# A fixed instruction order for every engine, with gated weight loads, an interleaved head and an unequal last tile

## The chip, the cores and the metric

The kernel runs on one core of a Trainium2 chip. The metric is the device time of that core in microseconds (us), lower is better. A kernel is timed in several executions; I quote the median and the range.

TensorE is called PE below, ScalarE is ACT, VectorE is DVE, GpSimd is POOL and SyncE is SP. "Full" matmuls use the whole 128x128 array. "Tiled" matmuls use it as four independent strips: the score fills take four heads side by side in four row strips, the products with the probabilities take them in four column strips.

## The reference, cut to what matters

The input x is 2048 x 512 in bf16. Two branches are mixed by a gate per token.

```python
g = sigmoid((x * gate_w).sum(-1, keepdims=True))
a = A(x, wq, wk, wv, wo, beta)          # 32 heads of 16, 4 segments of 512 tokens
b = (gelu(x @ w_gate) * (x @ w_up)) @ w_down     # 512 -> 1792 -> 512
return g * a + (1 - g) * b

# A, for each segment s of 512 tokens:
p = softmax(q_s @ k_s.T * scale + causal_mask)
a_dot = p @ v_s
a_mem = (phi(q_s) @ M) / (phi(q_s) @ z + 1e-6)   # memory of the earlier segments
o = sigmoid(beta) * a_mem + (1 - sigmoid(beta)) * a_dot
M += phi(k_s).T @ v_s;  z += phi(k_s).sum(tokens)
# A ends with o @ wo
```

Attention needs many exponentials on ACT (64 of 128x2048 elements and 8 for the low part of the mask) and, with 16 columns per head, tiled matmuls. The projections and branch B are full matmuls that fill the time between.

Of the kernel before, what the change touches and what calls it, by code (L numbers as in the profile page):

```python
# [32 lines left out]
PV_JOIN = 0.11  # L33
HOLD = 0.3
OPEN_BONUS = 6.0
BIAS = {
    "D0": -705, "D1": -805, "D2": -380, "D3": -442, "G0": -222, "G1": -900, "G2": -744, "G3": -86, "GdT0": 97,
    "GdT1": 844, "GdT2": -1, "GdT3": 895, "Gev0": 862, "Gev1": -349, "K0": 777, "K1": -529, "K2": 250,
    "K3": 307, "Q0": 715, "Q1": -519, "Q2": 584, "Q3": -641, "U0": -844, "U1": -888, "U2": -53, "U3": -206,
    "Um0": 900, "Um1": 148, "Um2": 49, "Um3": -86, "V0": 318, "V1": -357, "V3": 539, "Vev0": 540, "Vev1": 758,  # L40
    "Vev2": 262, "Vev3": -72, "Vlo0": -900, "Vlo1": 900, "Vlo2": -70, "Vlo3": 237, "consts": 21, "exp0": -666,
    "exp1": 177, "exp2": -517, "exp3": -395, "exsT0": 77, "exsT1": -899, "exsT2": -94, "exsT3": 695, "fin0": 37,
    "fin1": -471, "fin2": 741, "fin3": -517, "gbd": -146, "gelu0": -795, "gelu1": 416, "gelu2": 1, "gelu3": 126,
    "gexp": 402, "gexs0": -594, "gexs1": -701, "gexs3": 76, "gmat": -900, "gmul1": 900, "gmul2": -10,
    "gmul3": 319, "gsum0": -318, "gsum1": -86, "gsum2": -613, "gsum3": -900, "gts0": 73, "gts1": -850,
    "gts2": -487, "gts3": 848, "ident": 503, "kl0": -826, "kl1": -900, "kl2": -661, "kl3": 900, "kp0": 509,
    "kp1": 3, "kp2": -900, "kp3": -405, "masks": 769, "msk0": -290, "msk1": 789, "msk2": 116, "msk3": -63,
    "mz0": -162, "mz1": 638, "mz2": -319, "mzacc0": -423, "mzacc1": 170, "mzacc2": 439, "mzbd0": -25,
    "mzbd1": -178, "mzbd2": 70, "norm0": 704, "norm1": -880, "norm2": -46, "norm3": 166, "num2": -887,
    "num3": -200, "nump1": -900, "nump2": -220, "nump3": -164, "oTd1": 896, "oTd2": 268, "oTd3": 899,  # L50
    "omg": 528, "out0": 408, "out1": -644, "out10": 2, "out11": 869, "out12": 745, "out13": 461, "out14": -25,
    "out15": -280, "out2": 230, "out3": -27, "out4": 313, "out5": -134, "out6": 284, "out7": -18, "out8": 682,
    "out9": -139, "pkT0": 5, "pkT1": 569, "pkT2": 281, "pkc0": 489, "pkc1": -900, "pkc2": -14, "pke0": 310,
    "pke1": 399, "pke2": -73, "pqc1": 496, "pqc2": 14, "pqc3": -117, "pqe1": -17, "pqe2": 649, "pqe3": 63,
    "pv0": -95, "pv1": -551, "pv2": -900, "pv3": 30, "pvt0": -169, "pvt1": 86, "pvt2": -513, "pvt3": -26,
    "qk0": 417, "qk1": 185, "qk2": 503, "qk3": 669, "tload": 355, "vones": -877, "w": -765, "warm0": 21,
    "warm1": 747, "warm2": -324, "warm3": 371, "warm4": 223, "warm5": -120, "warm6": -334, "x0": -96,
    "x0ev0": 93, "x0ev1": 23, "x0t0": 596, "x0t1": 606, "x1": 367, "x2": -181, "x3": -900, "xt1": 533,
    "xt2": -189, "xt3": 11
}  # L60
HOP = {PE: 0.17, ACT: 0.07, DVE: 0.07, POOL: 0.10, SP: 0.0}
# [40 lines left out]
class Task:  # L102


    def __init__(self, name, alts, grp=None, after=(), bias=0.0, nbytes=0):
        self.name = name
        self.alts = alts
        self.grp = grp
        self.after = tuple(after)
        self.bias = bias + BIAS.get(name[:re.search(r"[_.]|$", name).start()], 0.0)  # L110
        self.nbytes = nbytes
        self.tiled = None
        self.patience = 0.0
        self.ahead = False
        self.est = {e: sum(i.est for i in l) for e, l in alts.items()}
        rs, ws = set(), set()
        for l in alts.values():
            for i in l:
                rs.update(i.reads)
                ws.update(i.writes)  # L120
        self.reads, self.writes = rs, ws
        self.preds, self.succs = set(), set()
        self.prio = 0.0
        self.eng = None
        self.start = self.finish = None
        self.id = None


class Sched:
# [32 lines left out]
    def schedule(self):  # L162
        tasks = self.tasks
        n = len(tasks)
        groups = defaultdict(list)
        for t in tasks:
            if t.grp is not None:
                groups[t.grp].append(t)
        for g in groups.values():
            for t in g[1:]:  # L170
                for d in () if t.ahead or PE in t.alts else t.preds:
                    if d.grp is not g[0].grp and d not in g[0].preds:
                        g[0].preds.add(d)
                        d.succs.add(g[0])
        indeg = [len(t.preds) for t in tasks]
        topo = [t for t in tasks if indeg[t.id] == 0]
        for t in topo:
            for s in t.succs:
                indeg[s.id] -= 1
                if indeg[s.id] == 0:  # L180
                    topo.append(s)
        assert len(topo) == n, "cycle"
        for t in reversed(topo):
            best = max([s.prio for s in t.succs] + [0.0])
            t.prio = min(t.est.values()) + best + t.bias
        npred = [len(t.preds) for t in tasks]
        ready_at = [0.0] * n
        ready = {e: set() for e in ENGINES}
        for t in tasks:
            if npred[t.id] == 0:  # L190
                for e in t.alts:
                    ready[e].add(t)
        cur = {e: 0.8 for e in ENGINES}
        bank_free = {b: 0.0 for b in range(self.nbanks)}
        dma_free = 0.0
        order = []
        last_pe = None
        while len(order) < n:
            best = None
            due = min([ready_at[t.id] for t in ready[ACT] if t.tiled == "exp"] + [1e9])  # L200
            held = sum(t.tiled == "pv" and ready_at[t.id] <= cur[PE] + HOLD for t in ready[PE])
            for e in ENGINES:
                for t in ready[e]:
                    st = max(cur[e], ready_at[t.id])
                    if e == ACT and t.tiled != "exp" and st + t.est[e] > due + 0.1:
                        continue
                    if t.tiled == "pv":
                        if last_pe in ("qk", "pv") and ready_at[t.id] <= cur[e] and bank_free and \
                                min(bank_free.values()) <= cur[e]:
                            if best is None or (-1.0, 0.0, t.id) < best[0]:  # L210
                                best = ((-1.0, 0.0, t.id), e, t)
                            continue
                        st += t.patience
                    if t.grp is not None and t.grp.bank is None:
                        if len(bank_free) <= (0 if t.tiled == "pv" else held):
                            continue
                        st = max(st, min(bank_free.values()))
                    open_ = t.grp is not None and t.grp.bank is not None
                    k = (st, -t.prio - (OPEN_BONUS if open_ else 0.0), t.id)
                    if best is None or k < best[0]:  # L220
                        best = (k, e, t)
            assert best is not None, "deadlock in task graph"
            (st, _, _), e, t = best
            if t.tiled == "pv":
                st = max(cur[e], ready_at[t.id], min(bank_free.values()))
            for a in t.alts:
                ready[a].discard(t)
# [5 lines left out]
            if e == PE:  # L233
                if t.tiled == "pv" and last_pe == "pv":
                    t.finish -= PV_JOIN
                last_pe = t.tiled
# [14 lines left out]
            for s in t.succs:  # L251
# [3 lines left out]
                if npred[s.id] == 0:  # L255
                    for a in s.alts:
                        ready[a].add(s)
# [116 lines left out]
def _build(es, nc, A_x, A_wq, A_wk, A_wv, A_wo, A_beta, B_w_gate, B_w_up, B_w_down, gate_w, out):  # L374
# [108 lines left out]
    rank = [9000.0]  # L483

    def xk(s, kb):

        return [("xT", s % NX, kb, u) for u in range(2)]

    def wdma(key, eng, dst, src, nbytes, nonc=False, after=()):
        rank[0] -= 20.0  # L490
        dma("w_" + str(key), eng, lambda: dst, lambda: src, [], [("w", key)], nbytes, bias=rank[0], nonc=nonc,
            after=after)

    def xdma(s, after=()):
        for kb in range(4):
            rank[0] -= 20.0
            dma(f"x{s}_{kb}", SP, lambda kb=kb: xT[s % NX][:, kb, :],
                lambda kb=kb: A_x[0, s * 512:(s + 1) * 512, kb * 128:(kb + 1) * 128],
                [], xk(s, kb), 262144, issue=1.25, transpose=True, bias=rank[0] if s < 2 else 0.0,
                after=after)  # L500
# [10 lines left out]
              [("c", "ident")], [("c", "ident")], 0.3)], bias=9990.0)  # L511
    task("tload", ACT, [Instr(lambda e: e.activation(stmp[:, 0:1], ones[:, 0:1], ACTF.Exp), writes=[("stmp",)],
                              est=1.5)], bias=8000.0)
    xin = hT[1][:, 0:4, :]
    for a in range(4):
        rank[0] -= 20.0
# [612 lines left out]
```

## The kernel before: the parts that the change and the argument touch

The kernel first builds a graph of tasks, then gives each engine its list of instructions. A task names what it reads and writes; semaphores follow from that. Before the change a list scheduler picks the order, with a hand-tuned bias per kind of task.

```python
BIAS = {"D0": -705, "D1": -805, "D2": -380, ...}          # [cut: 175 such biases in all]

def schedule(self):                                        # [cut to the choice]
    for t in reversed(topo):
        t.prio = min(t.est.values()) + max([s.prio for s in t.succs] + [0.0]) + t.bias
    while len(order) < n:
        for e in ENGINES:
            for t in ready[e]:
                st = max(cur[e], ready_at[t.id])
                if t.tiled == "pv":       # joined with a fill or another pv where it can be
                    if last_pe in ("qk", "pv") and ready_at[t.id] <= cur[e] and bank_free and ...:
                        ...
                    st += t.patience
                k = (st, -t.prio - (OPEN_BONUS if open_ else 0.0), t.id)
                if best is None or k < best[0]:
                    best = (k, e, t)
```

A score fill is 8 tiled matmuls (32 small ones for the low part of the mask) that write four PSUM banks ("X"), which one exp on ACT then reads. There is only one such set of banks, so the next fill can't start before the exp of the last one has ended. I call the time from fill to fill, when nothing but the exp holds it up, the exp round trip.

```python
def fill(name, steps, dst, key, masks):
    for (lhs, rhs, c0, ncol, rd) in steps:
        for g in range(4):
            e.matmul(X[g][:, c0:c0 + ncol], lhs(32 * g), rhs(32 * g),
                     start=True, stop=True, tile_position=(32 * g, 0))       # L803
    e.activation(dst[:], XALL[:, :].rearrange("p (g c) -> p g c", g=4),
                 ACTF.Exp, scale=ATT_SCALE)                                  # L810
    e.affine_select(out=view, ...)                                           # L814, POOL, the causal mask
```

A probability-times-value group ("PV") is 16 tiled matmuls with Vaug (L852) and 16 small ones for the low part (L860). The memory update is 64 small tiled matmuls (L769). Fills use row strips, PV groups and the memory update use column strips, so that PE has three modes: full, rows, columns. Each full matmul comes from one helper, line L449, and most are cut into pieces of two matmuls of 512 columns. The loads at the start and the end of the kernel:

```python
for a in range(4):                       # x0 in four row blocks on two issuing engines
    dma(f"x0_{a}", (SP, ACT)[a % 2], ..., A_x[0, a * 128:(a + 1) * 128, :], ...)
for c0, c1 in ((0, 128), (128, 512)):    # wk and wq in two column blocks
    for key, w, src in (("wk", wk, A_wk), ("wq", wq, A_wq)):
        wdma((key, c0 > 0), SP, w[:, :, c0:c1], r4(src)[:, :, c0:c1], ...)
...
for part in (dwn, att):                  # the last output tile: two halves of 256 columns
    for u in range(2):
        c0 = 256 * u
        ins = [mm(None, lambda u=u: X[u][:, 0:256], a, b[:, c0:c0 + 256], ...) ...]
# half 0 is copied out by ACT, half 1 by DVE; both are stored by SP
```

The softmax here doesn't subtract the row's maximum and nothing guards it: scores larger than these inputs give would overflow.

## Time and profile before

| | before |
|---|---|
| time, median of three runs | 269.23 us (269.0 to 269.25) |
| profiled span | 267.5 us |
| PE busy | 257.9 us (96%) |
| ACT busy / DVE busy | 212.1 us (79%) / 199.9 us (75%) |
| chain of waits that ended last | 84% PE |
| first score fill starts | 16.84 us |
| last matmul starts to end of span | 2.91 us |

The first lines are from the page of the kernel before: busy times by engine (time, share of the span, instructions), then the shares of the chain of work that ended last, then two groups of instructions (line, engine, operation, tiles, shapes, count | busy time, mean ns of one | idle time just before them and what ended it).

```profile
PE 257.9 (96%) x2965; PEld 118.4 (44%) x3005; DVE 199.9 (75%) x385; ACT 212.1 (79%) x188; POOL 102.3 (38%) x232
...
PE 84%; ACT 5%; DVE 3%; issue 3%; DMA 2%; POOL 1%; SPq 0%; ACTq 0%; DVEq 0%
...
L810 ACT ACTIVATE pt<-psXALL 128x2048 bf16<-128x2048 f32 x64 | 120.1, 1876 | 26.0 <-PE psXALL L803 23.9
```

PE has 2965 matmul records and 3005 weight loads: 40 matmul records are missing in this trace. "Issue" is time in which an engine waits for nothing that the profile shows. The Trainium skill ("Perfetto Trace Analysis", Identifying the Most-Contended Engine) warns that the busy share of matmuls is a poor measure of how close a kernel is to its limit, since they are pipelined. So I read PE from the start-to-start times of its instruction records.

Here is the wait view of PE of the kernel before (engine, tile, line, what it waited for: us in total, times, longest; one line and the last are cut).

```profile
PE psW L449 <- issue: 3.8, 24, 0.2
...
PE psW L449 <- ACT qT L463: 0.4, 1, 0.4
PE psW L449 <- ACT hT L937: 0.4, 1, 0.4
PE psXALL L803 <- ACT pt L810: 0.3, 2, 0.2
PE psW L449 <- DMA wk<-in_A_wk_dram: 0.3, 1, 0.3
```

PE hardly waits for a named source. The first line is no wait: its gaps stand where matmul records of 0.216 us are missing. The two waits of 0.4 us have a missing record in them as well. And this is how dense it is, in a stretch of the timeline of the kernel before in the last segment (start us, us, engine, line, operation, count, and an idle time in brackets if there was one).

```profile
227.26 0.40 PE L803 MATMUL psXALL<-qT,kpad 32*128 32x320 bf16 x8
227.59 2.33 PE L449 MATMUL psW<-xT,wu 128*128 128x512 bf16 x10
229.85 0.40 PE L803 MATMUL psXALL<-qT,kpad 32*128 32x448 bf16 x8
```

From one fill to the next are 2.59 us: ten full matmuls of 512 columns, 216 ns each, and a fill that takes 428 ns in all. The columns of the fill explain about 213 of the 428 ns. The other 0.2 us are what it costs to enter the tiled mode and leave it again, so about 0.1 us a switch. From row strips to column strips is a switch too: a PV group alone between full matmuls takes 0.76 us (read in the new order's trace, where single groups occur), a fill alone 0.43 us, and the two joined 1.09 us, which is one switch less than the sum.

### The profile page before, as it was taken

The numbers are of one execution on the slowest core, as the hardware profiler recorded it, in microseconds if no ns is written. First come the engines' busy times: TensorE is split into PE (matmuls) and PEld (weight loads), VectorE is DVE, ScalarE is ACT, GpSimd is POOL, SyncE is SP. The second block draws the span as 40 slices with busy tenths as digits, with TensorE's granted clock in tenths as the row PEclk, the third lists the DMA queues.
The fourth block names the chain that finished last, engine by engine and source line by source line (L and its number), as shares of the span: only waits on it lengthen the run. The fifth ranks groups of instructions, "written<-read, shape, count | busy, mean of one in ns | idle before, by whom it ended". The sixth has DMA issues, their size and how long they took to land.

```text
span 267.5 us, 7093 instructions
## 1 busy us (share of the span) xinstructions
PE 257.9 (96%) x2965; PEld 118.4 (44%) x3005; DVE 199.9 (75%) x385; ACT 212.1 (79%) x188; POOL 102.3 (38%) x232
## 2 busy tenths in 40 slices
PE   8999999999999999999999999999999999999996
PEld 5444444344443443434354444444344444444354
DVE  1769799898989898889756877987952688753451
ACT  4889988899998997998858998887767767777602
POOL 8364553873002433485201433486300252352300
PEclk9999999999999999999999999999999999999999
DMA  6998992000203443000021224010020025001002
GB/s 192 228 328 184 390 241 42 1 2 0 44 0 79 81 101 102 22 20 2 0 44 39 42 59 124 21 44 2 0 44 0 2 59 42 0 22 36 8 0 78
DMA packets 33775, 18.22 MB, mean 68 GB/s; under 512 B 21456, under 2 KB 33744, under 8 KB 33744
## 3 DMA queue, kind: packets, MB, share of 16 engines
q1 hardware_dynamic: 33456, 17.51, 27.0%
q8 instruction: 23, 0.38, 0.6%
q10 hardware_dynamic: 288, 0.26, 0.3%
q14 instruction: 8, 0.07, 0.1%
HBM read 9.84 MB, written 2.10 MB: 45 GB/s over the span
## 4 chain that ended last, share of the span: by engine, by line
PE 84%; ACT 5%; DVE 3%; issue 3%; DMA 2%; POOL 1%; SPq 0%; ACTq 0%; DVEq 0%
PE psW L449 68%; PE psXALL L803 8%; PE psW L852 5%; ACT pt L810 3%; DMA wk<-in_A_wk_dram 2%; PE psXALL L449 1%; PE psW L860 1%; POOL exsT L712 1%; DVE tb L867 0%; PE psW L769 0%; ACT L937 0%; ACT L926 0%; SPq L480 0%; DVE mzbd L784 0%; DVE phkt L692 0%
## 5 line engine op out<-in xcount | busy, mean ns | idle before, releaser
L810 ACT ACTIVATE pt<-psXALL 128x2048 bf16<-128x2048 f32 x64 | 120.1, 1876 | 26.0 <-PE psXALL L803 23.9
L814 POOL TENSOR_SCALAR_AFFINE_SELECT pt<-pt 128x256 bf16<-128x256 bf16 x128 | 59.2, 464 | 131.6 <-ACT pt L810 126.6
L449 PE MATMUL psW<-xT,wu 128*128 128x512 bf16 x216 | 51.9, 380 | 0.8 <-issue 0.6
L449 PE MATMUL psW<-xT,wg 128*128 128x512 bf16 x214 | 50.2, 380 | 1.7 <-issue 1.3
L449 PE MATMUL psW<-wd,hT 128*128 128x512 bf16 x203 | 50.3, 380 | 0.9 <-issue 0.8
L958 DVE TENSOR_TENSOR hT<-psW,hT 128x512 bf16<-128x512 f32 x56 | 37.5, 684 | 11.4 <-PE psW L449 10.9
L449 PEld LDWEIGHTS psW<-xT,wg 128*128 128x128 bf16 x224 | 20.4, 98 | 25.7 <-issue 2.5
L449 PEld LDWEIGHTS psW<-xT,wu 128*128 128x128 bf16 x224 | 20.4, 98 | 24.5 <-issue 2.3
L867 DVE STREAM_TRANSPOSE tb<-psW 128x512 f32<-128x512 f32 x32 | 21.3, 697 | 12.6 <-PE psW L860 12.2
L449 PEld LDWEIGHTS psW<-wd,hT 128*128 128x128 bf16 x210 | 18.8, 98 | 22.5 <-issue 2.5
L803 PE MATMUL psXALL<-qT,kpad 32*128 32x320 bf16 (+3 forms) x512 | 25.8, 273 | 0.3 <-ACT pt L810 0.3
L937 ACT ACTIVATE hT<-psW 128x512 bf16<-128x512 f32 x28 | 15.9, 601 | 7.0 <-PE psW L449 6.9
L814 POOL TENSOR_SCALAR_AFFINE_SELECT ptl<-ptl 128x2048 bf16<-128x2048 bf16 x8 | 16.9, 2117 | 9.4 <-ACT ptl L810 9.0
L803 PEld LDWEIGHTS psXALL<-qT,kpad 32*128 32x128 bf16 x512 | 7.7, 92 | 27.6 <-ACT pt L810 19.6
L852 PE MATMUL psW<-pt,vaug 128*17 128x192 bf16 (+3 forms) x512 | 18.7, 273 | 0.0
L810 ACT ACTIVATE ptl<-psXALL 128x2048 bf16<-128x2048 f32 x8 | 15.0, 1876 | 3.6 <-PE psXALL L803 3.6
L449 PE MATMUL psW<-xT,wk 128*128 128x512 bf16 (+1 forms) x64 | 16.1, 376 | 0.8 <-issue 0.5
L712 POOL COPY exsT<-exs 32x4 f32<-32x4 f32 x64 | 15.4, 241 | 3.7
L466 DVE CAST hT<-psW 128x512 bf16<-128x512 f32 x21 | 14.1, 683 | 2.8 <-PE psW L449 2.5
L449 PE MATMUL psW<-wo,oT 128*128 128x512 bf16 x55 | 15.2, 380 | 0.5 <-issue 0.3
L449 PE MATMUL psW<-xT,wq 128*128 128x512 bf16 x60 | 14.9, 380 | 0.7 <-ACT qT L463 0.4
L449 PE MATMUL psW<-wv,xT 128*128 128x512 bf16 x62 | 15.0, 380 | 0.3 <-issue 0.3
(98 smaller groups left out, 300.0 us busy)
## 6 DMA issues: line engine op xcount, KB each, us to landing
out_dram<-ost SPq DMA_DIRECT2D x15, 128.0 KB, 1.7
wg<-in_B_w_gate_dram SPq DMA_DIRECT2D x2, 896.0 KB, 6.1
wu<-in_B_w_up_dram SPq DMA_DIRECT2D x2, 896.0 KB, 5.9
wd<-in_B_w_down_dram SPq DMA_DIRECT2D x1, 1792.0 KB, 12.1
phkt<-in_A_x_dram SPq DMA_DIRECT2D x3, 512.0 KB, 4.1
vlow<-vaug SPq DMA_DIRECT2D x8, 136.0 KB, 2.9
wv<-in_A_wv_dram SPq DMA_DIRECT2D x1, 512.0 KB, 6.2
wo<-in_A_wo_dram SPq DMA_DIRECT2D x1, 512.0 KB, 9.7
```

The source lines that it names most:

```text
L449: return Instr(lambda e: e.matmul(view(), lhsT, rhs, start=first, stop=last), reads=reads, writes=[fkey if fkey is not None else g.key], e ...
L466: alts[DVE] = [Instr(lambda e: e.tensor_copy(dst(), src()), reads=reads, writes=writes, est=dve_t(n))]
L712: cross = task(f"exsT{s}", POOL, [Instr(lambda e, g=g, c=c: e.tensor_copy(exsT[sl][32 * g:32 * g + 32, c:16:4], exs[32 * c:32 * c + 32, s4 ...
L803: instrs.append(Instr(lambda e, g=g, lhs=lhs, rhs=rhs, c0=c0, ncol=ncol: e.matmul(X[g][:, c0:c0 + ncol], lhs(32 * g), rhs(32 * g), start=T ...
L810: prev_exp[0] = exp_task(s, f"exp{s}_{t}{name}", [Instr(lambda e: e.activation(dst[:], XALL[:, :].rearrange("p (g c) -> p g c", g=4), ACTF ...
L814: task(f"msk{s}_{t}{name}", POOL, [Instr(lambda e, view=view, pat=pat, base=base: e.affine_select(out=view, in_=view, compare_op=ALU.is_ge ...
L852: instrs.append(Instr(lambda e, t=t, q=q, kb=kb, slot=slot, c0=c0: e.matmul(gp.f32()[32 * q:32 * q + 17, 128 * kb + 64:512], Vaug[sl][:, k ...
L860: instrs.append(Instr(lambda e, t=t, q=q, kb=kb, c0=c0: e.matmul(gp.f32()[32 * q:32 * q + 17, 128 * kb:128 * kb + 64], Vlow[j][:, kb, 4 * ...
L867: task(f"pvt{s}_{t}_{j}", DVE, [Instr(lambda e: e.transpose(Tb[:, j, :], gp.f32()[:, :]), [gp.key], [("Tb", j)], dve_t(512))], grp=gp)
L937: lambda e, g=g, ft=ft, s=s: e.activation(hT[s % 2][:, ft, :], g.f32()[:, :], ACTF.Gelu_apprx_tanh),
L958: task(f"Um{s}_{ft}", DVE, [Instr(lambda e, g=g, ft=ft: e.tensor_tensor(hT[sl][:, ft, :], g.f32()[:, :], hT[sl][:, ft, :], ALU.mult), [g.k ...
```

## The change

Its intent is to replace the scheduler, which guesses, by a fixed list for each engine that was searched for with a better model of PE: it charges each change of mode, a slow clock in the first 5.8 us, and instruction fetch in blocks of 256. The large weights get gates, so that their transfers do not collide with the start. The head is cut finer.

```diff
-PV_JOIN = 0.11
+SWITCH = 0.097
+COLD = 5.8
+BLOCK, BLOCK_ASK, BLOCK_END = 256, 165, 208
-BIAS = { ... }
+ORDER = {"pe": ("warm3 warm0 warm2 warm1 warm6 warm4 x0t0_0 x0t1_0 warm5 K0_0.0 ..."),
+         "act": (...), "dve": (...), "pool": (...), "sp": (...)}     # [cut: lists of all tasks]
 def schedule(self):
-        # list scheduling with priorities                              [cut]
+        named = {t.name: t for t in self.tasks}
+        queue = {e: [named[x] for x in reversed(ORDER[e].split())] for e in ENGINES}
+        # takes each queue in order; only assigns the PSUM banks       [cut]

-    for c0, c1 in ((0, 128), (128, 512)):        # wk, wq by columns, after all of x0
-        for key, w, src in (("wk", wk, A_wk), ("wq", wq, A_wq)):
-            wdma((key, c0 > 0), SP, ...)
+    x0dma(0)
+    x0dma(1)
+    for kb in range(4):                          # wk by row blocks, on SP and ACT in turn
+        wdma(("wk", kb), (SP, ACT)[kb % 2], wk[:, kb, :], A_wk[128 * kb:128 * kb + 128, :], ...)
+    x0dma(2)                                     # issued as x0_0, wk0, x0_2, wk2 (SP)
+    x0dma(3)                                     #       and x0_1, wk1, x0_3, wk3 (ACT)

-        pieces(name, g, [mm(...) ...], 2 * nu)
+        pieces(name, g, [mm(...) ...], 1 if nu == 2 else 2)   # K of segment 0: 256-column pieces
+        # Q of segment 0 is accumulated in the score banks X                    [cut]

-                masks = [(PTl[:]..., [[0, 32], [2, 64]], 1, 2048)]
+                masks = [(PTl[:, g, :]..., [[0, 8], [2, 64]], 1, 512) for g in range(4)]

-    wdma(("wu", 0), SP, wu[:, :, 0:half], wur[:, :, 0:half], 917504, after=pk0)
+        wdma(("wu", i), SP, wu[:, :, sl], wur[:, :, sl], 917504, reads=[("tick", 0, *e)])
+    # likewise x2, wd in two halves, wo: each waits for the exp after a named fill of segment 0

-                        c0 = 256 * u
+                        c0, cn = 384 * u, (384, 128)[u]                # last output tile
```

The cut leaves out that wq and wv come in two halves each, and that x1 is loaded ahead of the second half of wg. The new PE list differs from the old order above all in how PV groups are placed. The old kernel always put two of them behind one fill. The new list often puts a single one beside a fill. Here is a stretch of the last segment, a "piece" being two matmuls of 512 columns:

```
before: qk3_1B0 pv3_0_0 pv3_0_1 (2 pieces) qk3_1A1 (5 pieces) qk3_1B1
after:  qk3_1B0 (3 pieces) pv3_0_0 qk3_1A1 (3 pieces) pv3_0_1 qk3_1B1
```

Here the two fills with their PV groups have five switches before and six after.

## The prediction

> **What bounds the kernel.** TensorE, issue after issue. The page gives PE 96% busy, ACT 79%, DVE 75%; the chain of waits that ended last is 84% PE. By the start-to-start times of the instruction records, a 512-column matmul starts 216 ns after the last one from 7.24 us to the last matmul at 264.6 us. The rest is structural: a score fill (8 row-tiled matmuls) costs 428 ns between full matmuls, of which about 213 are its own columns. So entering or leaving the tiled mode costs about 0.1 us. A fill joined with two probability-times-value (PV) groups saves one such switch (1.87 us, separately 0.43 + 1.54). Real stalls after 7.24 us come to only about 0.6 us, two of them (0.22 and 0.35 us) waits for an exp on ACT. Outside: 7.24 us of head, including 2.8 us of warm-up matmuls and a 0.45 us pause for wk (landed 7.19 us), and 2.9 us of tail after the last matmul starts.
>
> **What the change does.**
> 1. Head: wk in four row blocks among the x0 loads. wk should be in by about 5.5 us instead of 7.2, so the 0.45 us pause goes. But one warm-up now stands between the transposes (0.43 us at half clock): net about -0.2 us. The Trainium skill ("TensorE: Matmul & The Clock Gate", Part 1) says the array runs at half clock for its first few busy microseconds; the trace agrees (transposes 107 ns apart, full clock from 6.45 us).
> 2. Order: the matmul columns stay the same. Counting the new PE list, there are 173 mode switches; in the old trace I count 165, since PV groups were always joined in pairs. 8 x 0.1 = +0.8 us.
> 3. The old stalls (-0.6 us at best) can go. But five of the new fill-to-fill periods hold only 2.15 to 2.34 us by my sum, less than the exp round trip (2.46 us), four in the last segment: up to +0.8 us of new waits on ACT.
> 4. Gated weights: wu, wd, wo later. Needed only from about 67 us: no cost. The intent seems to be instruction fetch; the skill ("Runtime: NRT & Kernel Launch", Instruction fetch mechanics) describes 16 KiB blocks of 256 instructions; the trace shows 23 such packets on an instruction queue, about 1 us each. I find no PE stall there, so nothing to win.
> 5. Tail: the last piece on PE is now 384 columns evacuated by ACT (about 0.58 us, between 0.47 for 256 and 0.69 for 512) instead of 256 on DVE (0.48): about +0.1 us.
>
> **Sum.** +0.1 to +0.9 us, against the hope that a list from a better model stalls less than I see. Prediction 269.3 us, range 268.2 to 270.9. Faster by over 2%: 0.01; within 2%: 0.96; slower: 0.03.
>
> **What would show each step.** The first K projection matmul near 5.0 us and no wait on wk; PE work done by 12 us about 0.2 us ahead; 216 ns and 428 ns slots unchanged; PE waits on exp in the last segment's fills; last matmul to end about 3.0 us.
>
> **What would make it wrong.** Full clock granted earlier or later than 6.45 us (half of any shift is gained or lost); the fixed order meeting a late transfer (second half of wg, x1 in the first 20 us), which stalls everything behind it; fetch stalls where 300 instructions of tiled work follow each other fast; a cheaper switch from PV to a fill.

## The result, and the profile after

| | before | after |
|---|---|---|
| time, median | 269.12 us (268.83 to 269.25, 4 runs) | 270.23 us (270.02 to 271.0, 4 runs) |
| profiled span | 267.5 us | 268.5 us |
| PE busy | 257.9 us (96%) | 263.2 us (98%) |
| first score fill starts | 16.84 us | 14.79 us |
| last matmul starts to end of span | 2.91 us | 3.13 us |

The first fill starts 2.05 us earlier, but that is not a gain of this size: the new list has six matmuls of V (1.3 us) behind the first fill that the old one had before it. The ledger below takes this into account.

The ratio is 1.0048, with a 95% interval from 1.0026 to 1.007: within 2%, but slower beyond the noise. Ratios here are the mean time of one kernel's fast runs over that of the other's fast runs of the same rounds, so they are not quite the ratio of the medians in the table.

The page of the kernel after, in the same order as above:

```profile
PE 263.2 (98%) x3017; PEld 118.9 (44%) x3017; DVE 199.4 (74%) x387; ACT 213.1 (79%) x188; POOL 106.4 (40%) x256
...
PE 88%; ACT 9%; DMA 1%; issue 1%; POOL 0%; SPq 0%; ACTq 0%
...
L871 ACT ACTIVATE pt<-psXALL 128x2048 bf16<-128x2048 f32 x64 | 120.0, 1875 | 23.5 <-PE psXALL L864 21.4
L875 POOL TENSOR_SCALAR_AFFINE_SELECT ptl<-ptl 128x512 bf16<-128x512 bf16 x32 | 23.0, 719 | 77.3 <-ACT ptl L871 75.7
```

One exp still takes 1.88 us. (Most of the 5 us more of PE busy are the records that were missing before.) What is new is ACT in the chain: 9% instead of 5%. The wait view of PE of the kernel after:

```profile
PE psXALL L864 <- ACT pt L871: 0.8, 3, 0.3
PE psW L498 <- DMA wk<-in_A_wk_dram: 0.2, 1, 0.2
```

The waits for the exp rose from 0.3 to 0.8 us, and this view counts only the larger ones. Where they sit is plain in the chain of the kernel after, between 221 and 230 us (start us, us, what):

```profile
221.83 0.44 PE psXALL L864 x8
...
222.35 1.89 ACT pt L871
...
224.28 0.50 PE psXALL L864 x8
...
224.87 1.89 ACT pt L871
...
226.80 0.51 PE psXALL L864 x8
...
227.39 1.89 ACT pt L871
```

The chain goes from exp to fill to exp, every 2.52 us, and leaves the full matmuls out: this is the exp round trip. In the kernel before, the same chain from 223.91 us on runs through PE alone. The timeline of the kernel after shows why:

```profile
224.28 0.40 PE L864 MATMUL psXALL<-qT,kpad 32*128 32x320 bf16 x8 [0.17 <-ACT pt L871]
224.61 1.04 PE L498 MATMUL psW<-xT,wu 128*128 128x512 bf16 x4
225.49 0.59 PE L498 MATMUL psW<-wd,hT 128*128 128x512 bf16 x2
226.01 0.61 PE L914 MATMUL psW<-pt,vaug 128*17 128x448 bf16 x16
226.45 0.29 PE L922 MATMUL psW<-ptl,vlow 128*17 128x64 bf16 x16
226.80 0.40 PE L864 MATMUL psXALL<-qT,kpad 32*128 32x448 bf16 x8
```

This period holds six full matmuls (6 x 0.216 = 1.30 us) and a PV group joined with a fill, which takes 1.09 us where nothing stalls. That is 2.39 us of work in a period that the exp makes 2.52 us long. PE loses the other 0.13 us. By the starts of the fills, the old kernel's periods in this segment are mostly 2.59 us (five pieces and a fill) or 2.52 us (two pieces, two PV groups and a fill), and fit, the latter just so. One of them is too short as well: four pieces and a few small memory products, 2.27 us of work, which loses 0.25 us.

In the new list eight periods of the last segment hold less than a round trip. Four hold a single PV group and three pieces, about 2.38 us of work; they lose 0.14, 0.14, 0.14 and 0.08 us. Three hold four pieces and a few small memory products, 2.27 to 2.35 us; they lose 0.16, 0.19 and 0.25 us. One holds four pieces alone, 2.16 us, and loses 0.37 us. That makes 1.47 us, against 0.25 us in the old kernel.

### A ledger of PE's time

I summed the time between the starts of PE's records that its columns (N x 0.417 ns + 2.5 ns, fitted to the 216, 109 and 56 ns that the traces show for 512, 256 and 128 columns) and its mode switches (0.1035 us each, from single PV groups between full matmuls) do not explain. Two executions of each kernel were read this way; for the head, five of the old head and six of the new one, from the experiments that kept it. The residual of the model, about 0.9 us in all, is in the stalls of both columns. The time of the missing records of the first trace of before (39 after the first fill, 0.216 us each) is taken out of its stalls.

| us | before | after | difference |
|---|---|---|---|
| head: unexplained before the first fill, mean | 2.87 (2.59 to 3.18) | 2.89 (2.39 to 3.13) | 0.0 |
| mode switches, 165 and 173 | 17.08 | 17.91 | +0.83 |
| stalls after the first fill | 2.84 (2.65 and 3.02) | 3.35 (3.39 and 3.30) | +0.5 |
| of these in the last segment | 0.64 (0.64 and 0.64) | 1.76 (1.76 and 1.76) | +1.1 |
| last matmul starts to end | 2.91 | 3.13 | +0.22 |
| 12 more matmuls in K, 2.5 ns each | | | +0.03 |
| sum | | | about +1.6 |

The medians differ by 1.1 us in the first comparison and by 1.7 us in a later one, so the ledger fits in size. What it names had to be tested.

### The profile page after: what moved, and what is told of

Read it like the earlier page. It is cut to its first block, busy times and chain, and to the rows that moved or that the text cites. A ratio compares the mean times of both kernels' runs of the same rounds, so it can differ in the third digit from the quotient of the medians.

```text
span 268.5 us, 7148 instructions
## 1 busy us (share of the span) xinstructions
PE 263.2 (98%) x3017; PEld 118.9 (44%) x3017; DVE 199.4 (74%) x387; ACT 213.1 (79%) x188; POOL 106.4 (40%) x256
## 4 chain that ended last, share of the span: by engine, by line
PE 88%; ACT 9%; DMA 1%; issue 1%; POOL 0%; SPq 0%; ACTq 0%
PE psW L498 68%; PE psXALL L864 10%; ACT pt L871 7%; PE psW L914 5%; PE psXALL L498 3%; ACT ptl L871 1%; DMA wk<-in_A_wk_dram 1%; PE psW L922 1%; PE psW L830 1%; POOL ptl L875 0%; ACT ost L1050 0%; PE psXALL L596 0%; SPq L529 0%; ACTq L394 0%
## 5 line engine op out<-in xcount | busy, mean ns | idle before, releaser
L875 POOL TENSOR_SCALAR_AFFINE_SELECT pt<-pt 128x256 bf16<-128x256 bf16 x128 | 56.8, 454 | 67.2 <-ACT pt L871 62.4
L498 PE MATMUL psW<-xT,wu 128*128 128x512 bf16 x224 | 54.9, 380 | 0.0
L875 POOL TENSOR_SCALAR_AFFINE_SELECT ptl<-ptl 128x512 bf16<-128x512 bf16 x32 | 23.0, 719 | 77.3 <-ACT ptl L871 75.7
L498 PE MATMUL psW<-xT,wg 128*128 128x512 bf16 x224 | 53.6, 380 | 0.0
L498 PE MATMUL psW<-wd,hT 128*128 128x512 bf16 x210 | 52.5, 380 | 0.0
L498 PE MATMUL psW<-wv,xT 128*128 128x512 bf16 x64 | 17.0, 380 | 0.0
L498 PE MATMUL psW<-wo,oT 128*128 128x512 bf16 x60 | 16.1, 380 | 0.0
L773 POOL COPY exsT<-exs 32x4 f32<-32x4 f32 x64 | 14.4, 225 | 3.7
L914 PEld LDWEIGHTS psW<-pt,vaug 128*17 128x17 bf16 x512 | 10.2, 90 | 12.5 <-issue 4.9
L515 DVE CAST hT<-psW 128x512 bf16<-128x512 f32 x17 | 11.4, 684 | 2.6 <-PE psW L498 2.6
```

Source lines behind the costliest of these rows:

```text
L498: return Instr(lambda e: e.matmul(view(), lhsT, rhs, start=first, stop=last), reads=reads, writes=[fkey if fkey is not None else g.key], e ...
L515: alts[DVE] = [Instr(lambda e: e.tensor_copy(dst(), src()), reads=reads, writes=writes, est=dve_t(n))]
L773: cross = task(f"exsT{s}", POOL, [Instr(lambda e, g=g, c=c: e.tensor_copy(exsT[sl][32 * g:32 * g + 32, c:16:4], exs[32 * c:32 * c + 32, s4 ...
L875: task(f"msk{s}_{t}{name}", POOL, [Instr(lambda e, view=view, pat=pat, base=base: e.affine_select(out=view, in_=view, compare_op=ALU.is_ge ...
L914: instrs.append(Instr(lambda e, t=t, q=q, kb=kb, slot=slot, c0=c0: e.matmul(gp.f32()[32 * q:32 * q + 17, 128 * kb + 64:512], Vaug[sl][:, k ...
```

## The experiments

The theory: the change costs mode switches and new waits for the exp, a little at the tail, and wins nothing in the head. The rivals: the mask on POOL, now in four instructions, delays the low PV part; the gates let the weights come late; the cut of the last tile; the head and its clock; and instruction fetch. In the list that follows, "before" always means the runs of the kernel before on the same chip and in the same rounds, with medians of 269.14, 269.14 and 269.15 us in the three sessions.

| run | median us (range) | ratio to before, 95% interval |
|---|---|---|
| before_again | 269.03 (268.63 to 270.21) | 1.0002 (0.9984 to 1.002) |
| after_again | 270.82 (270.47 to 271.4) | 1.0059 (1.0028 to 1.009) |
| split8 | 270.98 (270.62 to 271.11) | 1.0065 (1.0049 to 1.008) |
| before_short | 267.35 (266.95 to 269.99) | 0.9947 (0.9915 to 0.9978) |
| after_short | 268.36 (268.05 to 268.54) | 0.9971 (0.9957 to 0.9985) |
| tail256 | 270.74 (270.43 to 271.34) | 1.0066 (1.0054 to 1.0078) |
| mask1 | 270.9 (270.78 to 271.26) | 1.0071 (1.0059 to 1.0083) |
| nogates | 270.41 (270.12 to 271.64) | 1.0044 (1.0016 to 1.0072) |
| x0first | 271.62 (270.87 to 273.38) | 1.0103 (1.0072 to 1.0133) |
| x0first2 | 270.73 (270.02 to 272.47) | 1.0057 (1.0025 to 1.0089) |
| oldorder | 271.81 (271.19 to 273.43) | 1.0107 (1.0086 to 1.0128) |
| shift128 | 268.63 (268.2 to 270.86) | 0.9983 (0.9949 to 1.0017) |

All of them passed the comparison with the reference.

### The two controls

Both kernels were run again without an edit, as before_again and after_again, which gave a second trace of each.

> The kernel before, unchanged, as a control. Both theories: 269.1 us, ratio 1.000 within 0.002. It tells (1) how far one execution's records may be trusted: in the first trace 40 of 3005 matmul records were missing, so the stalls summed from it are uncertain by some tenths of a us; and (2) whether the moment at which matmuls go to full rate (6.4 us in the old trace, before 4.9 us in the new) belongs to the kernel or varies from execution to execution. If it is chance, it should come at another time here, and up to 0.7 us of the new kernel's early lead is chance.

> The new kernel unchanged, beside the others on one chip: 270.0 to 270.9 us, ratio 1.004 to 1.007. The moment of full rate and the length of the head should differ again from its first trace (first score fill at 14.8 us there, 15.3 to 15.5 in three later traces of the same head).

The kernel before came out as before. The kernel after had 270.23 us in the first comparison and 270.82 us here. So its medians of two sessions differ by 0.6 us, and I do not read anything from a smaller difference between medians of different sessions. The traces, which show where each stall sits, are finer than that: the stalls by segment were 0.44, 0.38, 0.81 and 1.76 us in the first trace and 0.44, 0.28, 0.82 and 1.76 us in the second.

### split8: sixteen more mode switches in the old kernel

The old kernel with its own order written out, but eight of its pairs of PV groups are taken apart: the second group goes behind the next two matmuls. The work is the same.

```diff
-... qk1_2B0 pv1_1_0 pv1_1_1 D0_3.8 ...
+... qk1_2B0 pv1_1_0 D0_3.8 pv1_1_1 ...      # 8 times
```

> The old kernel with its whole order pinned, and in eight of its 16 PV pairs the second group moved behind the next two full matmuls: the same work, the same intervals between fills, 16 more mode switches. Theory A (a switch costs 0.10 us wherever it stands, so the new order's 8 more switches cost 0.8 us): +1.6 us over the old kernel, about 270.7, ratio 1.006. Rival (the 0.1 us is hidden as soon as other work is at hand): at most +0.3 us.

The time rose by 270.98 - 269.14 = 1.84 us for 16 switches, 0.115 us each; the interval of the ratio allows 1.3 to 2.2 us. The traces are closer: from the first fill to the last matmul split8 takes 249.75 us and before_again 248.11 us, which is 1.64 us or 0.10 us a switch, with about equal stalls (2.99 and 3.02 us). So the eight more switches of the new list cost 0.83 to 0.92 us, and this term of the ledger is shown. The Trainium skill ("TensorEngine Tiling (Array Packing)", Key Properties) says that a change of the tiling mode drains the engine; it gives no figure, and this is one for this kernel. Whether a drain is all of it no run here shows.

### before_short and after_short: a shorter exp in both kernels

From the third head group of the first segment on, the exp covers 384 of each 512 columns. PE's work is unchanged. The result is wrong, since the last columns keep old values. It passed the comparison all the same, which only shows that the comparison is wide there.

```diff
+                nx = 512 if s == 0 and t < 2 else 384
-                    dst[:], XALL[:, :].rearrange("p (g c) -> p g c", g=4), ACTF.Exp, ...
+                    dst[:, :, 0:nx], XALL[:, :].rearrange("p (g c) -> p g c", g=4)[:, :, 0:nx], ACTF.Exp, ...
```

> The old kernel with the same shortened exps and its order pinned. Theory A: the old order waits little for exp, so 0.3 to 0.7 us gained, near 268.6; what remains between this and the new kernel with short exps is switches (+0.8), tail (+0.2), head (-0.2) and the stall in the old kernel's long run of tiled instructions (0.35 to 0.7 us in two traces). Rival (both orders are bound by exp alike): gains as much as the new kernel does.

> The new kernel with each exp, after the first eight row fills and their low fill, over 384 of 512 columns per group (wrong result on purpose): 1.88 us becomes about 1.45. Theory A (about 2.4 us of the new kernel are TensorE waits for exp, 1.4 of them in the last segment): these waits vanish, total about 2 us below the new kernel, near 268.3. Rival (the waits are harmless because TensorE would wait for something else right after): less than 0.7 us gained.

Two lines of the page of after_short: the chain, and the group of the exps.

```profile
PE 88%; DVE 7%; issue 2%; DMA 2%; SPq 0%; ACT 0%; DVEq 0%; ACTq 0%
...
L872 ACT ACTIVATE pt<-psXALL 128x1536 bf16<-128x1536 f32 (+1 forms) x64 | 96.2, 1503 | 39.3 <-PE psXALL L865 38.0
```

With 1.45 us for a shortened exp (the 1503 ns are a mean with eight full ones in it), ACT is gone from the chain. The stalls of the new order fell from 3.35 to 0.86 us, and the time to 268.36 us. The old order gained too, more than I had thought: its stalls fell from 2.84 to 1.31 us and its time by 1.79 us to 267.35 us. Without the exp as a limit the new order is still 268.36 - 267.35 = 1.01 us slower. That this is about the switches and the tail alone (0.83 + 0.22 us) is chance: the new order has 0.45 us less of stalls here, and in the profiled executions, which differ by 1.08 us, its head happened to be 0.5 us longer.

The stalls can now be split. The old traces hold a stall that is put down to instruction fetch below, of 0.53 us in the mean; before_short has one of 0.36 us. Waits that a shorter exp removes are then 2.49 us in the new order (3.35 - 0.86) and 1.36 us in the old one ((2.84 - 0.53) - (1.31 - 0.36)): +1.1 us. The new order has no fetch stall: -0.5 us. The rest is 0.86 against 0.95 us: -0.1 us. The sum is the +0.5 us of the ledger. The new list did remove old stalls, as was hoped, and put larger ones in their place.

### tail256: equal halves in the new order

```diff
-                        c0, cn = 384 * u, (384, 128)[u]
+                        c0, cn = 256 * u, 256                  # in both places
```

> The new kernel with its last output tile cut in 256 and 256 columns again, order untouched. Theory A (the 384/128 cut costs, because the wide piece is the last on TensorE and its evacuation and store are longer): last matmul to end falls from 3.16 us towards 2.9 to 3.0, total 0.1 to 0.25 us faster than the new kernel. Theory B (the cut is free or helps): same or slower.

The time from the last matmul to the end was 3.10 us, as with the unequal cut (3.13), not 2.91 us as in the old kernel. The time, 270.74 us (ratio 1.0066), is no lower than that of the new kernel either. So the cut is not the cost. The copy on ACT became shorter (0.47 instead of 0.58 us), but the last store then waited for the issue of the one before it (266.50 to 266.93 us) and took longer to issue. These are the ends of the chains of the kernel before and of the kernel after:

```profile
261.36 3.51 PE psXALL L449 x32
264.89 0.48 DVE obf L990
```

```profile
264.05 1.64 PE psXALL L498 x10
265.79 0.58 ACT ost L1050
```

In the new list the last piece on PE is the one that ACT copies out; in the old one it is the one for DVE. That the order of the last pieces is what costs the 0.2 us is argued from these lines; no run changed it alone.

### mask1: the low mask in one instruction again

The chain of the new kernel holds POOL steps (`ptl`), and its page shows 23.0 us for the four-part mask.

```diff
-                masks = [(PTl[:, g, :].rearrange("p (b c) -> p b c", c=64), [[0, 8], [2, 64]], 1, 512)
-                         for g in range(4)]
+                masks = [(PTl[:].rearrange("p g (b c) -> p (g b) c", c=64), [[0, 32], [2, 64]], 1, 2048)]
```

> The new kernel with the mask of the low tile in one POOL instruction of 2048 columns again instead of four of 512 (2.12 us against 4 x 0.72 us in the two traces). If POOL is on the way of the exp chain, as a piece of the new chain of waits suggests (POOL ptl, 0.67 us), 0.2 us or more faster; if that is only an attribution, no change (within 0.1 us).

270.9 us (ratio 1.0071), against 270.82 us of after_again (1.0059, in another session), and stalls of 3.35 us in all: no difference that shows. POOL's place in the chain was where the chain passed, not what bounded it.

### nogates: the weights without their gates

```diff
-        wdma(("wu", i), SP, wu[:, :, sl], wur[:, :, sl], 917504, reads=[("tick", 0, *e)])
+        wdma(("wu", i), SP, wu[:, :, sl], wur[:, :, sl], 917504)      # likewise x2, wd, wo
```

> The new kernel with wu, x2, wd and wo no longer gated by score fills, lists untouched. Theory A (gates neither cost nor save, since these weights are used from 67 us on): within 0.3 us of the new kernel. Rival (the gates keep bulk loads out of the way of TensorE's instruction fetches): 0.5 us or more slower, with stalls inside tiled runs between 22 and 45 us.

270.41 us beside 270.82 us of after_again in the same session, with intervals that overlap, and stalls of 3.28 us beside 3.30 us. The gates neither cost nor win anything that shows.

### x0first and x0first2: the head without interleaving

The first edit issues all of x0 before wk, as the old kernel did. The second also moves the second transposes on PE ahead of the K pieces.

```diff
-"x0_0 w_wk0 x0_2 w_wk2 ..."   (SP)      "x0_1 w_wk1 x0_3 w_wk3 ..."   (ACT)
+"x0_0 x0_2 w_wk0 w_wk2 ..."   (SP)      "x0_1 x0_3 w_wk1 w_wk3 ..."   (ACT)
 # x0first2 also, on PE:
-x0t0_0 x0t1_0 warm5 K0_0.0 K0_1.0 K0_3.0 K0_1.1 K0_3.1 K0_0.1 x0t0_1 x0t1_1
+x0t0_0 x0t1_0 x0t0_1 x0t1_1 warm5 K0_0.0 K0_1.0 K0_3.0 K0_1.1 K0_3.1 K0_0.1
```

> The new kernel with the interleave undone: all four x0 loads before the four wk row blocks on the two queues, every other list as it is. In the new kernel's four traces x0's second half lands at 5.0 to 6.3 us (old kernel: 4.0 to 4.3) and the last wk block at 6.2 to 7.2 us (old: 6.9 to 7.2), and the second half of the transposes waits for x0. Theory A (the interleave gains little, since it delays x0 by as much as it brings wk forward): x0 lands by 4.4 us, wk by about 7, the first score fill starts no later, total within 0.3 us of the new kernel. Rival (the interleave is what the head gains): 0.5 us or more slower.

x0first failed as a test. The PE list still had six K pieces ahead of the second transposes, so everything waited for wk at 5.8 to 6.0 us. In its profiled execution the full clock came only at 10.35 us, and the head lost 5.30 us instead of about 2.9.

> The interleave undone together with the order that belongs to it: x0's four loads first, all 16 transposes together, then one warm-up, then K. The first try (loads alone) failed as a test: K pieces that wait for wk stand before the second transposes, and full rate came only at 10.4 us. Theory A (interleave is worth little): x0 by 4.3 us, wk 5.8 to 6.7 us, first score fill at 15.0 to 15.6 us, total within 0.3 us of the new kernel. Rival (the interleave carries the head): first fill 0.5 us or more later.

With the order on PE put right, the loads behaved as in the old kernel: x0 was in by 4.2 us, wk between 5.64 and 6.49 us, the first K matmul started at 5.78 us instead of 4.8 to 5.2 us, and the first fill at 15.51 us. The traces with the new head (and the new order after it) have their first fill at 14.79, 15.14, 15.35, 15.40, 15.49 and 15.53 us. So the later start was made good, and the total, 270.73 us, is the same as after_again's. I conclude that the interleaving is worth nothing that these runs can show. It brought the first wk block in at 4.1 to 5.1 us, but the last at 6.4 to 7.2 us (6.6 to 7.2 us in the old head), and the second half of x0 at 5.0 to 6.3 us instead of by 4.3 us: what wk gained, x0 lost.

What moves the head more is the clock. From the spacing of the matmuls, the full clock began at 3.8 us in two executions (before_short, after_again) and at 6.9 us in another (x0first2), with others between, and once at 10.35 us. The kernel before had 6.45 us in its first trace and 4.0 us in the second. The Trainium skill ("TensorE: Matmul & The Clock Gate", Part 1) says that the window in which the activity is measured is free-running, so that the moment depends on where in it the kernel starts. The traces agree that it varies between executions of one kernel; the spread here is larger than the plus or minus 500 ns that the page states for sustained activity. In the first trace of the kernel before PE ran almost without a pause from 0.84 us on, and the full clock came 5.6 us later.

### oldorder: the new head with the old order behind it

The new lists up to the first score fill, then the old kernel's own order on each engine.

```diff
 ORDER["pe"] = "warm3 ... V0_3.0 V0_1.0 V0_1.2 V0_3.2 qk0_0A0"
-              " V0_1.0 V0_1.2 G0_2.0 G0_2.2 V0_3.2 qk0_0B0 Q1_1.0 ..."
+              " Q1_0.0 Q1_0.2 Q1_1.0 G0_10.0 G0_10.2 qk0_0B0 G0_11.0 ..."   # as the old kernel ran
```

> The new kernel's head (its list for every engine up to the first score fill, its loads of x0, wk, wq, wv) and after that the old kernel's order on every engine, with the new tail cut, the new mask and the new gates. Theory A (the new order is what costs: 8 more mode switches and about 1 us more waiting for exp, while the head gains 0.8 us): 173 switches become 165, waits on exp in the last segment fall from 1.7 us to about 0.9, total about 268.6 us, faster than both kernels. Theory B (gates, mask or tail cost the time, the order is harmless): 270 us, like the new kernel.

This was a surprise: with 165 switches, a head of 3.08 us and only 0.64 us of stalls in the last segment, it should have been at about the time of the kernel before. It took 271.81 us, so as a test of the order alone it failed. In its trace, which is of the slowest of its six executions, the stalls are 5.17 us, and two of them stand out that are no wait for an exp. The timeline of oldorder around the first, and its wait view:

```profile
100.21 0.25 PE L926 MATMUL psW<-ptl,vlow 128*17 128x64 bf16 x9
101.67 0.23 PE L926 MATMUL psW<-ptl,vlow 128*17 128x64 bf16 x7 [1.21 <-issue]
```

```profile
PE psW L926 <- issue: 1.2, 1, 1.2
PE psXALL L868 <- issue: 0.8, 1, 0.8
```

PE stops in the midst of a PV group, waiting for nothing that the profile shows. The place is the longest tiled run of the segment: a fill, the memory update and two PV groups follow each other, 136 small matmuls with 136 weight loads, 272 instructions in 2.0 us where nothing stalls. On the instruction queue a packet of 16 KB ran from 98.92 to 100.29 us, and PE went on at 101.67 us, 1.4 us after its end. At the next memory update it was the same, this time in the fill just behind the run: a packet from 163.03 to 164.75 us, PE on at 166.01 us. The larger gaps that I read from the record starts were 1.40 and 1.11 us.

The same stall is in the kernel before, smaller. From the timeline of before_again:

```profile
97.40 0.40 PE L803 MATMUL psXALL<-qT,kpad 32*128 32x320 bf16 x8
97.73 0.71 PE L769 MATMUL psW<-vaug,phkt 128*32 128x34 bf16 x64
...
98.89 0.62 PE L852 MATMUL psW<-pt,vaug 128*17 128x448 bf16 x16
...
100.10 0.36 PE L803 MATMUL psXALL<-qT,kpad 32*128 32x448 bf16 x2
100.81 0.39 PE L803 MATMUL psXALL<-qT,kpad 32*128 32x448 bf16 x6 [0.35 <-issue]
```

Here the packet ran from 98.24 to 99.39 us, and the fill behind the run and two full matmuls broke off after two matmuls until 100.81 us: 0.71 us lost by the starts. In the first trace of the kernel before it was 0.35 us, until 100.70 us, and before_short and split8, which keep this stretch of the old order, break off at the same matmul, for 0.36 and 0.72 us. The Trainium skill ("Runtime: NRT & Kernel Launch", Instruction fetch mechanics) describes blocks of 256 instructions, fetched in sequence, and calls the cost of a block's boundary "mostly hidden". Counting PE's instructions, the long run began at number 142 of a block in the kernel before, at 166 and 130 for the two in oldorder (whose head has 24 instructions more), and at 226 for its counterpart in the new order, which did not stall. The second such run of the kernel before began at 106 and did not stall either. By the same count PE stopped at instruction 166 in before_again, and at 168 and 158 in oldorder. So the place in the block may decide, which could be tested.

Of the 4.1 us by which the profiled span of oldorder (271.7 us) exceeds that of before_again (267.6 us), the stalls are 2.2 us and the tail is 1.7 us. In the tail, 4.62 us instead of 2.91, the last two stores were issued at 267.70 and 268.08 us and landed at 270.97 and 271.17 us, some 3.2 us later instead of about 1.6. A packet of the instruction queue ran at the same time; whether it was the cause stays open. The other five executions, which have no trace, had spans of 269.2 to 270.2 us: not all of this happens in each run, but they too lie 1.5 us or more above those of the kernel before (266.9 to 267.7 us). Why is open.

### shift128: the old kernel, its instructions moved within the blocks

To test the fetch, the old kernel's order is written out, and sixteen of its early groups of four matmuls of 512 columns (all of G0, and two of G1) are made of eight of 256. These are 64 more matmuls and 64 more weight loads, 128 instructions, before the first memory update with two PV groups. Half a block is the largest shift there is.

```diff
-        ins = [mm(g, lambda: g.f32()[:, :], wg[:, kb, ...], xT[x3][:, kb, :], ..., 512) for kb in range(4)]
+        # s == 0, and ft 0, 1 of s == 1: two halves of 256 columns, all kb for each
+        e.matmul(g.f32()[:, 256*u:256*u+256], wg[:, kb, ...], xT[x3][:, kb, 256*u:256*u+256], ...)
```

> The old kernel, order pinned, with 64 full matmuls of the first gate projection cut in two halves of 256 columns: no new work (64 x 2.5 ns = 0.16 us), but everything after stands 128 instructions (64 weight loads and 64 matmuls) later in TensorE's stream. Theory A (the stall inside the longest tiled run, 0.35 and 0.71 us in two traces, is instruction fetch: the run of 272 instructions meets the edge of a 256-instruction block; it began at 142 of a block; with the old order behind the new head it began at 166 and at 130 and stalled 1.40 and 1.11 us): the run now begins at 14 of a block, the stall is gone, total 0.2 to 0.5 us faster than the old kernel, about 268.8. Rival (the stall is a data wait that the profile misses): the stall stays, total 0.1 to 0.2 us slower.

The run now began at instruction 14 of a block, and at 234 the second time. The timeline of shift128 at the same place:

```profile
97.33 0.40 PE L717 MATMUL psXALL<-qT,kpad 32*128 32x320 bf16 x8
97.66 0.71 PE L683 MATMUL psW<-vaug,phkt 128*32 128x34 bf16 x64
...
99.50 0.60 PE L363 MATMUL psW<-xT,wk 128*128 128x512 bf16 x2
100.04 0.40 PE L717 MATMUL psXALL<-qT,kpad 32*128 32x448 bf16 x8
```

The stall is gone: the fill of eight runs through. The stalls of the segment fell to 0.90 us, from 1.22 and 1.59 us in the two traces of before, and those of the whole kernel to 2.33 us, though 128 instructions were added. The profiled span is 266.8 us. So the place of a dense run within the fetch blocks matters, which agrees with the page's account of blocks of 256, and the stall was real: four traces with the run at 142 have it, the one trace with the run at 14 has not. In time, five of six runs lie between 268.2 and 268.66 us, one at 270.86 us; the interval of the ratio includes 1. It has the lowest median of the correct versions, but I can't call it faster than the kernel before.

## Why the prediction was right or wrong

The forecast "within 2%" and the range (268.2 to 270.9 us) held: 270.23 us. That says little for the sum, since the range is 2.7 us wide and 270.82 us in the second session was near its edge. The centre was 0.9 us too low: +0.1 us was predicted, +1.1 us measured at first and +1.7 us later. Point by point:

1. **The bound.** Right. (Two of its figures, 1.87 and 1.54 us, are 0.22 us too long: a record is missing behind these PV pairs in the first trace. In before_again they come to 1.65 and, by the columns and switches, 1.31 us. The saving of one switch is not touched by it.) PE issues back to back, and every change of the list that gives it more switches or shorter periods shows in the time.
2. **Head, predicted -0.2 us: measured none.** The failing step was "wk should be in by about 5.5 us instead of 7.2". The last block of wk landed at 6.4 to 7.2 us and the second half of x0 later than before. The first K matmul did start near 5.0 us, as predicted, but no time was left of that by the first fill: the unexplained time in the head has a mean of 2.89 us with the new head and 2.87 us with the old. The warning about the clock was right; it moves the head by more than the edit.
3. **Switches, predicted +0.8 us: right.** 173 against 165 gives +0.83 us, and split8 shows the price, at 0.10 us a switch by its trace and 0.115 us by its time.
4. **Stalls, predicted -0.6 us and up to +0.8 us: the mechanism was right, the sizes off.** The new waits are where they were announced, in the last segment. But its stalls rose from 0.64 to 1.76 us, and waits that depend on the length of the exp rose by 1.1 us in all. Two terms were mis-sized. The four periods that I had counted there ("2.15 to 2.34 us by my sum") lost 0.97 us (0.16 + 0.19 + 0.25 + 0.37), since the round trip is 2.52 us, not the "2.46 us" of the prediction; 0.25 us of this the old order lost too. And the four with a single PV group, about 2.38 us, were not among those that I counted; they lost another 0.50 us. The old stalls, on the other hand, were more than "-0.6 us at best" (2.65 us in the trace that I had), and of them about 0.6 us went: 0.5 us of fetch and 0.1 us of others.
5. **"I find no PE stall there, so nothing to win": wrong.** The stall of fetch was in the trace that I had, 0.35 us until 100.70 us in its record starts, in the midst of a fill. I had looked only for the waits that the views name. The "0.35 us" that the prediction puts down to an exp may be this very stall: the two waits for an exp above 0.2 us that the starts show in that trace are 0.22 and 0.24 us. Moving the blocks took it away (shift128). I had, however, named "fetch stalls where 300 instructions of tiled work follow each other fast" as a risk, and that is the place.
6. **Gates, predicted no cost: right** (nogates).
7. **Tail, predicted +0.1 us: measured +0.22 us.** The copy on ACT was sized rightly (0.58 us). But tail256 shows that the width is not the cost.
8. **The sum.** The terms gave "+0.1 to +0.9 us", and I took the low end, for "the hope that a list from a better model stalls less than I see". That was 0.4 of the 0.9 us by which the centre missed: a hope is not a term. The middle of my own sum would have been 269.7 us.

Where the expected gain went: the new list did take away the fetch stall (0.5 us) and other old stalls (0.1 us), and it gave back 1.1 us in exp waits and 0.8 us in switches. Single PV groups do both: taking a pair apart costs a switch or more, and the periods that then hold one group and three pieces are shorter than the round trip. What stays open: the new list with its short periods filled up (one more piece in each) was not run, so that the repair is only argued; nor is it known why a mode switch costs 0.1 us, or what made the tail of oldorder long.

## What to carry to other kernels

Where one engine issues back to back, price a new order by counting: mode switches times the price read from a slot, and, for each period between two users of a single buffer, the work in it against the round trip of the consumer. Here a period that was shorter by 0.1 us lost 0.1 us each time, and the view of waits hid most of it, while start-to-start times of the records show it. Look for stalls without a named cause inside and just behind the densest runs of small instructions. Read how much a head varies between traces that share it (0.6 and 0.7 us here) before promising a gain there. And where records are missing from a trace, take their time out before calling it a stall.

## What the Trainium skill lacked or had wrong

- "TensorEngine Tiling (Array Packing)" says that a mode switch drains the engine, without a price. Here it was 0.1035 us by the record starts of single groups, 0.10 us by the trace of split8 and 0.115 us by its time.
- "Runtime: NRT & Kernel Launch" (Instruction fetch mechanics) calls the cost of a block's boundary "mostly hidden" and says that the pace of issue hides the fetch. With 272 instructions in 2.0 us it did not: stalls of 0.35, 0.71, 1.40 and 1.11 us, ending 1.3 to 1.4 us after the packet's end, and none when the run stood elsewhere in its blocks (14 and 234 instead of 142). The page does not say that the place within a block matters.
- "TensorE: Matmul & The Clock Gate" (Part 1) gives plus or minus 500 ns for the start of the full clock, at about 4 us of sustained activity. Here it lay between 3.8 and 6.9 us (3.0 and 6.1 us after the first matmul), and once, where PE waited for loads, at 10.35 us. The same part also calls the number of slow matmuls run-variable, which fits.
